# Attention and two gated MLPs in one kernel: streamed sums of squares, normalisations placed earlier in the schedule, and the first loads of v on another queue

## The chip, the cores and the metric

One Trainium2 chip, one core of it. The metric is the time of one execution on the device in microseconds (us). A measurement gives the median of several runs; a profiled execution gives a span, the granted clock of the matrix engine, and a row for every instruction.

## The reference

Causal attention with a decay bias for 4 batches x 8 heads, 576 positions, head size 64, then a gated MLP behind an RMS normalisation, then a second gated MLP without one. Everything is float32; the tokens are 2304, the model width 512, the hidden width 1536.

```python
scores = scale * q @ k.T                      # per batch and head, scale = 1/8
cum = cumsum(maximum(s, 0))
bias = -(cum[:, None] - cum[None, :])
scores = where(causal, -1e9, scores + minimum(bias, 0))
attn = exp(scores - max(scores)); attn /= sum(attn) + 1e-9
x = (attn @ v)                                # then heads side by side: 2304 x 512
xn = x / sqrt(mean(x * x) + 1e-6) * rms_g
h = silu(xn @ w_gate) * (xn @ w_val); x = h @ w_out
h = silu(x @ w2_gate) * (x @ w2_val); out = h @ w2_out
```

## The kernel before

The program writes no fixed order of instructions by hand. Each step is registered with `op(engines, cost in ns, function, what it reads, what it writes, priority)`. `Plan.run` then plays the whole kernel through once with these costs: each engine takes the ready step with the lowest priority value, a step that lists several engines goes to one of them, and the order that comes out is the order in which the instructions of each engine stand in the program. On the chip the engines follow that order; a step that waits holds up what stands behind it on the same engine. A DMA costs SP 450 ns or bytes / 350 per ns, whichever is more, and its data counts as landed 2300 ns plus bytes / 350 after its start; `later` adds to that for those who need it (2500 ns for the weights).

The engines: PE is the matrix engine, ACT the scalar engine, DVE the vector engine, POOL the general engine, SP the engine that issues nearly all DMAs. ACT can issue DMAs too.

Numbers of float32 are split into two float32r parts, high and low (`H` and `L`), and most products are made as three products of parts. The queries of each batch form two groups: A is positions 0 to 255, B is 256 to 575.

The stages that the change touches lie in the first 460 us or so:

- `attend_early`: group A of batches 0 and 1, 16 heads (`EarlyUnit`). For each head SP loads q and k (`lq`, L858) and v (`vl`, L866), 128 KB and 64 KB. PE makes scores (L874; L880 adds the bias for the first four heads), DVE and ACT make the exponentials (L669, L680), PE transposes them (L890), ACT or DVE evicts the transposes (`pTA`, L895), PE multiplies with v (L900), and ACT or DVE stores the result in `x` (L905).
- Beside it SP loads the weights of the first MLP in pieces of 512 KB (`raw`, L430). They arrive as 8-byte numbers; ACT (L433), DVE (L435), ACT or POOL (L440, L441) and POOL or DVE (L444) make the two parts of them.
- `attend`: group B of batches 0 and 1, then both groups of batches 2 and 3, with masks on POOL (L657, L761), scores L643, minima on DVE (L669), transposes L712, parts on ACT and DVE (L715, L717) and products with v (L724). The splits of q, k and v (L595, L598, L607) go to POOL or DVE.
- `normalise`, once for each group of each batch, eight times. ACT squares `x` in four pieces `k` of 128 rows, two heads each (L926, into `sq`, two buffers). PE sums the squares of each head for each token (L932): the squares are the stationary operand, 128 tokens at a time, and a two-column selector `half` streams, so a piece takes two matmuls for group A and three for B. DVE makes the factor of each token and head from the sums in 20 small steps (L960 to L994), PE transposes the factors (L998), ACT evicts them (L1001), PE spreads each over the 64 rows of its head with the selector `sel` (L1006), and DVE multiplies `x` by it (L1010). ACT and POOL or DVE split the result (L1013, L1015).
- `moe1`: for 12 pieces of the hidden width and each group, 24 matmuls for gate and value (L1026, `gate_value`), with 256 or 320 columns, then L1033, L1035 and L1038, and a store to `h_d` (L1066). These have a high priority value and fill PE wherever the attention leaves it free.
- `sums_of_rows`: from about 315 us on SP loads rows of `h_d` back (`tb`), DVE makes differences of them (L1310) and SP stores these.

Four banks of PSUM (`mo`) are shared by the gate and value matmuls and the normalisations. From about 460 us on come the output product of the first MLP and the second MLP.

The order around the change is set by the priorities:

```python
normalise(x, "A", tot, P_ATT + len(units))           # in attend_early
...
for g, x, tot in zip(gs, xs, tots):                  # in attend
    normalise(x, g, tot, P_ATT + len(units))
...
moe1([(1, "B", 1)], W1, P_ATT + 36, -1.0e4)
```

Of the kernel before, what the change touches and what calls it, by code (L numbers as in the profile page):

```python
# [43 lines left out]
def f32(ap):  # L44
    return ap.bitcast(F32)
# [34 lines left out]
class Plan:  # L80
# [19 lines left out]

    def op(self, eng, ns, fn, r=(), w=(), pri=0.0, later=0, port=False):

# [7 lines left out]
        if eng == SP:  # L110
            took = ns / self.RATE
            ns = max(450.0, took)
            done = 2300.0 + took - ns
        deps, shared = set(), []
# [186 lines left out]
def tile_kernel(  # L301
# [73 lines left out]

    half = buf("m1", "half", [P, 2], F32)
    sel = buf("m1", "sel", [P, 2 * KD, D], F32R)

    totals = [buf("m1", f"tot{i}", [P, 3, NH], F32) for i in range(4)]


    sq = [buf("m1", f"sq{i}", [P, (320, 384)[i]], F32) for i in range(2)]
    tot3 = [buf("m1", f"tt{i}", [P, NH // 2], F32) for i in range(2)]
    xbuf = [buf("m1", f"x{i}", [P, KD, 320], F32) for i in range(2)]
# [17 lines left out]
    def convert(src, dst, c, stage, y, pri, early=None, after=()):  # L402
# [19 lines left out]
        def whole(dtype=F32):  # L422
# [8 lines left out]
            out=stage().bitcast(U16)[:, :4 * n - 1], in_=src.bitcast(U16)[:, 1:]),  # L431
           r=after, w=[stage], pri=pri if early is None else early, later=2500)
        op(ACT, c_act(n) + 165, lambda en: en.activation(  # L433
# [40 lines left out]
    def setup():  # L474
# [34 lines left out]
        def cumulate(out, n, pri, after=()):  # L509
            rows = NB * NH  # L510
            cum2 = buf("at", "cb0" if after else "cvt0", [rows, S], F32, "cum2")

# [12 lines left out]
        def later():  # L525
            def selectors(en):
                for j in range(2):
                    en.memset(half()[64 * j:64 * j + 64, j:j + 1], 1.0)
                    en.memset(half()[64 * j:64 * j + 64, 1 - j:2 - j], 0.0)
                en.tensor_tensor(  # L530
                    out=sel()[:],
                    in0=ident()[:, 0:NH].rearrange("p (h o) -> p h o", o=1).to_broadcast([P, NH, D]),
                    in1=ident()[:, NH:2 * NH].rearrange("p (h o) -> p h o", o=1).to_broadcast([P, NH, D]),
                    op=ALU.add)
            op([(POOL, 1800), (DVE, 1200)], 0, selectors, r=[ident, "early 1"], w=[half, sel], pri=3.5)

# [290 lines left out]
    class EarlyUnit(Unit):  # L827
# [28 lines left out]
        def load(self, pri):  # L856
# [5 lines left out]
            if not self.first:  # L862
                op(SP, 1024, lambda en: en.dma_start(
                    out=ql()[D:D + 1, 1, 288 * i:288 * i + 256], in_=cumA()[n:n + 1]),
                   r=[cumA, self.rows], w=self.parts[2:], pri=pri, later=1000)
            op(SP, 512 * P, lambda en: en.dma_start(out=self.v(), in_=vp[self.b, self.h, :, 0:2]),  # L866
               w=[self.vl], pri=pri)

# [43 lines left out]

    def normalise(i, g, tot, pri):

# [5 lines left out]
        ps = mo_bank()  # L920

        def squares():
            return ps()[:, :nt * NH].rearrange("p (t h) -> p t h", h=NH)
        for k in range(KD):
            q = sq[k % 2]
            op(ACT, c_act(n) + 35, lambda en, q=q, k=k: en.activation(  # L926
                q()[:, :n], x()[:, k, :n], ACTF.Square),
               r=[(x, (k, 0)), (x, (k, 64))], w=[q], pri=pri)

            def sums(en, q=q, k=k):  # L930
                for c in range(nt):
                    en.matmul(squares()[:, c, 2 * k:2 * k + 2], q()[:, at[c]:at[c] + P], half(),  # L932
                              start=True, stop=True)
            op(PE, 206 * nt, sums, r=[q, half], w=[ps], pri=pri)
        col = ring("m1", "rc", 2, [P, 3, 3], F32)
# [152 lines left out]
    def attend_early(b, x, tot):  # L1088
        for h in range(NH):
# [6 lines left out]
            if u.i == 3:  # L1096
                later()
        normalise(x, "A", tot, P_ATT + len(units))

    def attend(b, gs, xs):  # L1100
# [31 lines left out]
        for g, x, tot in zip(gs, xs, tots):  # L1132
            normalise(x, g, tot, P_ATT + len(units))

# [15 lines left out]
    moe1([(0, "B", 0)], W1, P_MOE + 100, -1.0e4)  # L1150
    moe1([(1, "B", 1)], W1, P_ATT + 36, -1.0e4)
    for b in range(2, NB):
# [681 lines left out]
```

## Time and profile before

| | |
|---|---|
| three runs | 1069.13, 1073.40 and 1074.58 us, median 1073.4 |
| the profiled execution | 1078.08 us, span 1076.3 us |
| mean granted clock of PE | 0.994 of full speed |
| busy: PE, DVE, ACT, POOL | 1051.4, 778.9, 634.4, 234.4 us |
| DMA | 211.16 MB, mean 196 GB/s |

Times below are counted from the span's start. Busy time on PE counts pipelined matmuls, so a row's duration is longer than the distance to the next one; prices of matmuls are therefore read from the chain of waits, where the pieces follow each other without overlap. A float32 matmul that is not split stands in the trace as two records.

### The profile page before, as it was taken

Reading aid. Unit: us, or ns where it says so; the run is one execution under the profiler, and the core shown is the slowest. Engines: PE = TensorE matmul, PEld = TensorE weight load, DVE = VectorE, ACT = ScalarE, POOL = GpSimd, SP = SyncE. Lnnn points to the kernel's source line nnn. Section 1 sums busy time; section 2 is a strip of 40 time slices with the busy share of each in tenths; the row PEclk is TensorE's granted clock in tenths of the full one; section 3 lists DMA queues with packets and bytes.
Section 4 is the critical chain, followed back from the end, with each engine's and each line's share of the span. In section 5 each row is a group of like instructions: output and inputs, shape, how many; then the busy total and the mean of one; then the engine's idle time right before and its main releaser. Section 6 shows DMA issues by size and latency. Waiting matters only on the chain.

```text
span 1076.3 us, 19524 instructions
## 1 busy us (share of the span) xinstructions
PE 1051.4 (98%) x6372; PEld 947.4 (88%) x6372; DVE 778.9 (72%) x1882; ACT 634.4 (59%) x1355; POOL 234.4 (22%) x322
## 2 busy tenths in 40 slices
PE   7989999999998999999999999999999999999998
PEld 5689999999998999999987889888888888878888
DVE  6888887866787876666777889566657776876453
ACT  5879767856762675332455766545556544664552
POOL 4158634522331341000000000122112221200000
PEclk9999999999999999999999999999999999999999
DMA  6786645433447751566588673565766658877773
GB/s 175 256 273 183 182 139 151 145 100 100 122 132 238 231 159 37 188 194 210 186 268 270 204 223 98 192 223 197 247 218 238 234 195 282 284 259 244 229 226 118
DMA packets 127382, 211.16 MB, mean 196 GB/s; under 512 B 16112, under 2 KB 55024, under 8 KB 127280
## 3 DMA queue, kind: packets, MB, share of 16 engines
q1 hardware_dynamic: 127232, 209.84, 61.5%
q8 instruction: 50, 0.82, 0.3%
q14 instruction: 52, 0.43, 0.1%
q10 hardware_dynamic: 48, 0.07, 0.0%
HBM read 145.29 MB, written 64.56 MB: 195 GB/s over the span
## 4 chain that ended last, share of the span: by engine, by line
PE 75%; DVE 10%; DMA 6%; ACT 4%; issue 3%; SPq 1%; POOL 0%; DVEq 0%; ACTq 0%; POOLq 0%
PE mo L1026 20%; PE mo L1565 9%; PE mo L1395 8%; PE sps L1565 7%; PE tp L724 4%; PE tp L1395 4%; PE sps L1395 4%; PE mo L1641 2%; PE tp L712 2%; PE sps L643 2%; PE sps L1026 2%; PE tp L1026 2%; PE mo L1450 2%; DMA raw<-in_w_gv 2%; DMA tb<-h_d 1%
## 5 line engine op out<-in xcount | busy, mean ns | idle before, releaser
L1026 PE MATMUL mo<-xL,H 128*128 128x256 f32 (+1 forms) x672 | 203.1, 302 | 1.1 <-DVE xL L1015 0.9
L1026 PE MATMUL mo<-xH,H 128*128 128x256 f32 (+1 forms) x672 | 202.6, 303 | 0.1
L1026 PE MATMUL mo<-xH,L 128*128 128x256 f32 (+1 forms) x672 | 202.2, 301 | 0.0
L1291 DVE TENSOR_TENSOR hL<-hh,hH 128x512 fp32r<-128x512 f32 (+1 forms) x192 | 124.1, 662 | 74.0 <-ACT hH L1288 73.8
L1288 ACT ACTIVATE hH<-hh 128x512 fp32r<-128x512 f32 (+1 forms) x192 | 114.3, 602 | 94.7 <-DVE hL L1291 13.8
L1026 PEld LDWEIGHTS mo<-xL,H 128*128 128x128 f32 x672 | 128.5, 191 | 1.9 <-DVE xL L1015 1.2
L1026 PEld LDWEIGHTS mo<-xH,H 128*128 128x128 f32 x672 | 128.4, 191 | 0.8 <-ACT xH L1013 0.3
L1026 PEld LDWEIGHTS mo<-xH,L 128*128 128x128 f32 x672 | 128.5, 191 | 0.1
L680 ACT ACTIVATE sc<-sc,col 128x128 f32<-128x128 f32 (+3 forms) x128 | 73.1, 572 | 58.3 <-DVE col L669 57.4
L1395 PE MATMUL mo<-hH,wo 128*128 128x512 f32 x312 | 98.1, 390 | 0.4 <-ACT hH L1288 0.4
L1395 PEld LDWEIGHTS mo<-hH,wo 128*128 128x128 f32 x312 | 58.6, 188 | 13.1 <-ACT hH L1288 1.1
L1033 ACT ACTIVATE t<-mo 128x256 f32<-128x256 f32 (+1 forms) x84 | 34.0, 405 | 59.9 <-PE mo L1026 59.6
L1395 PE MATMUL mo<-hL,wo 128*128 128x512 f32 x156 | 61.1, 391 | 0.6 <-DVE hL L1291 0.4
L1395 PE MATMUL tp<-hH,wo 128*128 128x512 f32 x192 | 60.4, 389 | 0.0
L1035 DVE SCALAR_TENSOR_TENSOR t<-t,mo 128x256 f32<-128x256 f32 (+1 forms) x84 | 37.9, 451 | 30.7 <-ACT t L1033 30.1
L1571 ACT ACTIVATE u<-sps 128x512 f32<-128x512 f32 x48 | 28.5, 594 | 51.7 <-PE sps L1565 49.8
L724 PE MATMUL tp<-pTB,vst 128*128 128x320 f32 (+2 forms) x320 | 52.4, 295 | 2.1 <-DVE pTB L717 1.4
L1395 PE MATMUL sps<-hH,wo 128*128 128x512 f32 x168 | 53.2, 390 | 0.5 <-ACT hH L1288 0.5
L724 PEld LDWEIGHTS tp<-pTB,vst 128*128 128x128 f32 x320 | 46.5, 189 | 5.0 <-DVE pTB L717 3.7
L717 DVE TENSOR_TENSOR pTB<-tp,pTB 128x512 fp32r<-128x512 f32 x64 | 44.0, 688 | 8.6 <-ACT pTB L715 7.7
L1038 DVE TENSOR_TENSOR hh<-t,mo 128x256 f32<-128x256 f32 (+1 forms) x84 | 37.8, 450 | 14.7 <-PE mo L1026 13.3
L712 PE MATMUL tp<-ident,sc 128*128 128x128 f32 x304 | 47.1, 274 | 0.2 <-DVE park L798 0.2
(272 smaller groups left out, 2861.8 us busy)
## 6 DMA issues: line engine op xcount, KB each, us to landing
raw<-in_w_gv SPq DMA_DIRECT2D x44, 511.8 KB, 5.3
tb<-h_d SPq DMA_DIRECT2D x48, 256.0 KB, 3.5
t<-tb SPq DMA_DIRECT2D x48, 256.0 KB, 2.2
hh<-t SPq DMA_DIRECT2D x48, 256.0 KB, 3.2
lq<-in_qk SPq DMA_DIRECT2D x32, 288.0 KB, 3.6
cb<-cum_d SPq DMA_DIRECT2D x32, 288.0 KB, 3.6
hh<-h_d SPq DMA_DIRECT2D x36, 256.0 KB, 3.3
h_d<-hh SPq DMA_DIRECT2D x54, 128.0 KB, 2.2
```

Source lines behind the costliest of these rows:

```text
L680: op(ACT, c_act(o + m, 2) + 35, lambda en: en.activation(sc()[:m, :o + m], sc()[:m, :o + m], ACTF.Exp, scale=-1.0, bias=col()[:m, 0, t:t + 1],
L712: op(PE, C_TR, lambda en, pt=pt, a=a, kb=kb, t=t: en.transpose(pt()[:, a * P:a * P + P], self.sc[t]()[:, kb * P:kb * P + P], ident()), r=[ ...
L717: op(DVE, c_tt(n), lambda en, pt=pt, c=c: en.tensor_tensor(out=place(L, c), in0=source(pt, c), in1=f32(place(H, c)), op=ALU.subtract), r=[ ...
L724: op(PE, c_mm(n), lambda en, w=w, z=z, kb=kb, d0=d0, n=n, o=o: en.matmul(po()[:, o:o + n], vst[j]()[:, kb, :], pT[g][z]()[:, d0:d0 + n], s ...
L1026: op(PE, c_mm(n), lambda en, a=a, x=x, c=c, k=k, i=i: en.matmul(ps()[:, :n], a()[:, c], x()[:, k, :n], start=(k == 0 and i == 0), stop=(k ...
L1033: op(ACT, c_act(n), lambda en: en.activation(t()[:, :n], gp()[:, :n], ACTF.Tanh, scale=0.5), r=[gp], w=[t], pri=pri)
L1035: op(DVE, c_tt(n), lambda en: en.scalar_tensor_tensor(out=t()[:, :n], in0=t()[:, :n], scalar=1.0, in1=gp()[:, :n], op0=ALU.add, op1=ALU.mu ...
L1038: op(DVE, c_tt(n), lambda en: en.tensor_tensor(out=hh()[:, :n], in0=t()[:, :n], in1=vp_()[:, :n], op=ALU.mult), r=[vp_, t], w=[hh], pri=pri)
L1288: op(ACT, c_act(n) + 35, lambda en: en.activation(H(), src(), ACTF.Copy), r=[src, *after], w=[H], pri=pri)
L1291: lambda en: en.tensor_tensor(out=L(), in0=src(), in1=f32(H()), op=ALU.subtract),
L1395: op(PE, c_mm(n), lambda en, m=m, w=w, xx=xx, kk=kk, i=i: en.matmul(ps[m]()[:, :n], w(), xx(), start=first and kk == 0 and i == 0, stop=kk ...
L1565: op(PE, c_mm(n), lambda en, w=w, xx=xx, cut=cut, kk=kk, i=i: en.matmul(ps()[:, :n], W[w]()[:, cut], xx(), start=first and kk == 0 and i == 0,
```

## The change

Six of the eight normalisations (all but those of `attend_early`) sum the squares in another way. Each piece of squares is split into a high part (`sqH`, on POOL or ACT) and a low part (`sqL`, on DVE or POOL). The parts stream through PE, with a window of the selector `zsel` as the stationary operand: 72 columns wide, of which only the two columns of this piece's heads hold ones. Eight matmuls of 256 or 320 columns add up in one bank, eight heads by tokens; ACT or DVE evicts the sums, PE transposes them into a second bank, 128 tokens at a time, and the small steps go on from there. `zsel` is made in `selectors`.

Every normalisation's priority value is lowered by 2, that of group A in `attend` by 1 more, and that of the gate and value work of batch 1, group B, is raised from 36 to 40. The loads of v of the first four early heads are issued by ACT's queue, ahead of everything else there but the load of s. The schedule counts the weights of the first five pieces (ten transfers) as landing 1500 ns later.

```diff
-    def op(self, eng, ns, fn, r=(), w=(), pri=0.0, later=0, port=False):
+    def op(self, eng, ns, fn, r=(), w=(), pri=0.0, later=0, port=False, slow=0.0):
...
-            done = 2300.0 + took - ns
+            done = 2300.0 + took - ns + slow
...
+    zsel = buf("m1", "zsel", [P, 72 + 2 * KD - 2], F32R)
+    sqs = buf("ex", "ex2", [P, 1024], F32R, "sqs")
+    sqH = [Part(sqs, i, lambda t, i=i: t[:, 320 * i:320 * i + 320]) for i in range(2)]
+    sqL = Part(sqs, 2, lambda t: t[:, 640:960])
...
-           r=after, w=[stage], pri=pri if early is None else early, later=2500)
+           r=after, w=[stage], pri=pri if early is None else early, later=2500,
+           slow=0.0 if early is None or early > P_ATT - 986 else 1500.0)
...
+                en.memset(f32(zsel()), 0.0)
+                for j in range(2):
+                    en.memset(f32(zsel()[64 * j:64 * j + 64, 2 * KD - 2 + j:2 * KD - 1 + j]), 1.0)
...
-            op(SP, 512 * P, lambda en: en.dma_start(out=self.v(), in_=vp[self.b, self.h, :, 0:2]),
-               w=[self.vl], pri=pri)
+            if self.first:
+                op(ACT, 450, lambda en: en.dma_start(
+                    out=self.v(), in_=vp[self.b, self.h, :, 0:2]), w=[self.vl], pri=pri - 1e6)
+            else:
+                op(SP, 512 * P, lambda en: en.dma_start(
+                    out=self.v(), in_=vp[self.b, self.h, :, 0:2]), w=[self.vl], pri=pri)
...
-    def normalise(i, g, tot, pri):
+    def normalise(i, g, tot, pri, split=True):
+        pri -= 2
...
-            def sums(en, q=q, k=k):
-                for c in range(nt):
-                    en.matmul(squares()[:, c, 2 * k:2 * k + 2], q()[:, at[c]:at[c] + P], half(),
-                              start=True, stop=True)
-            op(PE, 206 * nt, sums, r=[q, half], w=[ps], pri=pri)
+            if not split:
+                def sums(en, q=q, k=k):
+                    for c in range(nt):
+                        en.matmul(squares()[:, c, 2 * k:2 * k + 2], q()[:, at[c]:at[c] + P], half(),
+                                  start=True, stop=True)
+                op(PE, (206 * nt, 2), sums, r=[q, half], w=[ps], pri=pri)
+                continue
+            qh = sqH[k % 2]
+            op([(POOL, c_pts(n)), (ACT, c_act(n) + 35)], 0, {
+                ACT: lambda en, q=q, qh=qh: en.activation(qh()[:, :n], q()[:, :n], ACTF.Copy),
+                POOL: lambda en, q=q, qh=qh: en.tensor_scalar(
+                    out=qh()[:, :n], in0=q()[:, :n], scalar1=1.0, scalar2=1.0, op0=ALU.mult,
+                    op1=ALU.mult)}, r=[q], w=[qh], pri=pri)
+            op([(DVE, c_tt(n)), (POOL, c_ptt(n))], 0, lambda en, q=q, qh=qh: en.tensor_tensor(
+                out=sqL()[:, :n], in0=q()[:, :n], in1=f32(qh()[:, :n]),
+                op=ALU.subtract), r=[q, qh], w=[sqL], pri=pri, port=True)
+
+            def sums(en, qh=qh, k=k):
+                for z, part in enumerate((qh, sqL)):
+                    en.matmul(ps1()[:72, :n], zsel()[:, 2 * (KD - 1 - k):2 * (KD - 1 - k) + 72],
+                              part()[:, :n], start=k + z == 0, stop=k + z == KD)
+            op(PE, 2 * c_mm(n), sums, r=[qh, sqL, zsel], w=[ps], pri=pri)
+        if split:
+            op([(ACT, c_act(n)), (DVE, c_tt(n))], 0, {
...
+               r=[ps], w=[sq[0]], pri=pri)
+            ps2 = mo_bank()
+            for c in range(nt):
+                op(PE, C_TR, lambda en, c=c: en.transpose(
+                    ps2()[:, c * P:c * P + P], sq[0]()[:, at[c]:at[c] + P], ident()),
+                   r=[sq[0], ident], w=[ps2], pri=pri)
+            ps = ps2
...
-        normalise(x, "A", tot, P_ATT + len(units))
+        normalise(x, "A", tot, P_ATT + len(units), False)
...
-            normalise(x, g, tot, P_ATT + len(units))
+            normalise(x, g, tot, P_ATT + len(units) - (1.0 if g == "A" else 0.0))
...
-    moe1([(1, "B", 1)], W1, P_ATT + 36, -1.0e4)
+    moe1([(1, "B", 1)], W1, P_ATT + 40, -1.0e4)
```

How it moves the instructions is shown at three places. The line numbers of the changed kernel are larger: L866 is the load of `lq` there, L875 that of `vl` on ACT, L434 that of the weights, L950 the sums as before, L966 the streamed sums, L1051 the spreading with `sel`, L1071 gate and value.

First the start of SP's queue, before the change from its fifth transfer on (ahead of it stands the same pair of `lq` and `vl` twice):

```order
L858 DMA lq_118<-in_qk 64x2x256
L866 DMA vl_122<-in_vp 128x128
L858 DMA lq_110<-in_qk 64x2x256
L866 DMA vl_146<-in_vp 128x128
L430 DMA raw_168<-in_w_gv 128x2047
L858 DMA lq_118<-in_qk 64x2x256
L430 DMA raw_180<-in_w_gv 128x2047
```

and now from its third on (ahead of it two loads of `lq`):

```order
L866 DMA lq_118<-in_qk 64x2x256
L866 DMA lq_110<-in_qk 64x2x256
L434 DMA raw_152<-in_w_gv 128x2047
L434 DMA raw_168<-in_w_gv 128x2047
L866 DMA lq_118<-in_qk 64x2x256
L434 DMA raw_180<-in_w_gv 128x2047
```

The loads of `vl`, four among the first eight transfers, are gone, and the first load of weights stands fifth instead of ninth.

The same time on ACT, up to the second conversion of weights (`cvy`), before:

```order
L480 DMA cum<-in_s 32x576
L680 ACT_TABLE_LOAD
L680 ACTIVATE sc_172,tot_126<-sc_172,col_173 128x128
L680 ACTIVATE sc_182,tot_126<-sc_182,col_173 128x256
L680 ACTIVATE sc_188,tot_126<-sc_188,col_189 128x128
L433 ACTIVATE cvy<-raw_168 128x512
L895 ACTIVATE pTA_208<-tp_186 128x384
L433 ACTIVATE cvy<-raw_180 128x512
```

and now, from the third of four loads of `vl` on, the load of `cum` ahead of them all:

```order
L875 DMA vl_122<-in_vp 128x128
L875 DMA vl_141<-in_vp 128x128
L688 ACT_TABLE_LOAD
L688 ACTIVATE sc_174,tot_127<-sc_174,col_175 128x128
L688 ACTIVATE sc_184,tot_127<-sc_184,col_175 128x256
L688 ACTIVATE sc_190,tot_127<-sc_190,col_191 128x128
L438 ACTIVATE cvy<-raw_152 128x512
L907 ACTIVATE pTA_209<-tp_188 128x384
L438 ACTIVATE cvy<-raw_168 128x512
```

The four loads of `vl` stand ahead of the table load; the eviction `pTA` of the first head still stands behind the first conversion of weights.

The third place is PE in the normalisations of the last batch, from the spreading of group A on (`sel`), with group B's sums of squares beside it, before:

```order
L1026 MATMUL mo_6300<-xH_1384,L_535 128x320
L1006 MATMUL mo_6324<-xL_638,sel 128x256
L1006 MATMUL mo_6326<-xL_638,sel 128x256
L932 MATMUL mo_5945<-half,sq_124 128x2 x3
L932 MATMUL mo_5945<-half,sq_304 128x2 x3
L1006 MATMUL mo_6348<-xL_638,sel 128x256
L1006 MATMUL mo_6351<-xL_638,sel 128x256
L932 MATMUL mo_5945<-half,sq_124 128x2 x3
L1026 MATMUL mo_6361<-xH_1384,H_612 128x320
L1026 MATMUL mo_6361<-xL_1327,H_612 128x320
```

and now:

```order
L1071 MATMUL mo_6434<-xH_1297,L_733 128x320
L1051 MATMUL mo_6464<-xL_642,sel 128x256
L1051 MATMUL mo_6468<-xL_642,sel 128x256
L966 MATMUL mo_6365<-sqs,zsel 72x320 x2
L1051 MATMUL mo_6477<-xL_642,sel 128x256
L1071 MATMUL mo_6486<-xH_1297,H_808 128x320
L1071 MATMUL mo_6486<-xL_1245,H_808 128x320
L1071 MATMUL mo_6486<-xH_1297,L_879 128x320
```

Before, nine sums with two columns (`half`) stand between and behind the four spreading matmuls; now there are two streamed sums (`zsel`) between them, and the next two pairs follow after 14 and 19 more gate and value matmuls.

## Rows read from the trace of the kernel before

**Rows 1.** Busy us by stretch: PE, PEld, DVE, ACT, POOL; then clock, DMA share, GB/s.

```profile
0.00:60.00 60.00, 50.58 (x271) 38.40 (x272) 46.40 (x162) 45.33 (x127) 18.96 (x33) 0.95 0.75 226
60.00:90.00 30.00, 28.18 (x219) 27.35 (x218) 25.37 (x87) 23.40 (x55) 19.86 (x25) 0.99 0.83 261
60.00:400.00 340.00, 331.00 (x2496) 323.16 (x2495) 268.96 (x898) 230.91 (x577) 144.70 (x229) 0.99 0.55 164
```

**Rows 2.** Who PE waited for, whole span: us in total, times, longest us.

```profile
PE sps L874 <- POOL mask L504: 3.8, 1, 3.8
PE tp L900 <- ACT pTA L895: 3.6, 2, 2.4
PE mo L1006 <- DVE hh L1038: 1.8, 1, 1.8
PE mo L932 <- ACT sq L926: 1.2, 1, 1.2
```

**Rows 3.** Busy us by stretch, three stretches in which the granted clock is low.

```profile
57.00:60.60 3.60, 3.60 (x18) 3.60 (x18) 3.54 (x11) 2.98 (x7) 0.82 (x1) 0.53 0.99 321
343.60:347.20 3.60, 3.53 (x17) 3.53 (x18) 3.06 (x8) 0.89 (x3) 0.00 (x0) 0.54 0.60 224
431.50:435.00 3.50, 3.50 (x19) 3.50 (x19) 2.60 (x13) 1.39 (x5) 0.67 (x1) 0.66 0.84 277
```

**Rows 4.** Line 932, its matmuls: duration ns min/median/max, first and last start.

```profile
L932 PE MATMUL mo<-half,sq x160: 165/251/272, 22.0 to 431.6; 128*128 128x2 f32 x160
```

**Rows 5.** The chain that ended last: start us, us, what, instructions.

```profile
289.42 0.79 PE mo L932 x8
349.14 0.44 PE tp L712 x4
349.58 0.34 PE mo L932 x4
...
479.92 3.52 PE mo L1026 x24
513.83 2.88 PE tp L1026 x24
```

**Rows 6.** Timeline of the start, SP's queue, then ACT: start us, us, instruction.

```profile
0.73 0.68 SPq L858 DMA_DIRECT2D lq<-in_qk  x1
5.75 0.43 SPq L430 DMA_DIRECT2D raw<-in_w_gv  x1
...
1.14 1.28 ACT L680 ACT_TABLE_LOAD   x1 [1.14 <-PEq L1824]
5.93 0.40 ACT L680 ACTIVATE sc<-sc,col 128x128 f32<-128x128 f32 x1 [3.50 <-DVE col L669]
11.60 0.77 ACT L433 ACTIVATE cvy<-raw 128x512 f16<-128x512 bf16 x1 [2.75 <-DMA raw<-in_w_gv]
12.25 0.46 ACT L895 ACTIVATE pTA<-tp 128x384 f32<-128x384 f32 x1
```

**Rows 7.** Busy us by stretch at the start.

```profile
3.00:4.50 1.50, 0.68 (x2) 0.50 (x2) 1.44 (x2) 0.00 (x0) 1.31 (x4) 1.00 0.52 146
10.50:12.70 2.20, 0.00 (x0) 0.00 (x0) 0.95 (x6) 1.10 (x2) 0.00 (x0) 1.00 1.02 321
12.70:16.20 3.50, 3.44 (x9) 2.37 (x10) 1.92 (x2) 2.37 (x8) 1.94 (x2) 0.51 0.30 103
```

**Rows 8.** Tiles `raw` (the weights' transfers) in the first 70 us, issue to landing.

```profile
DMA to landing us min/median/max: 3.9/5.3/7.3
```

**Rows 9.** Timeline of DVE in batch 2's normalisations.

```profile
333.66 1.42 DVE L1310 TENSOR_TENSOR tb<-tb 128x512 f32<-128x512 f32 x2 [2.22 <-DMA tb<-h_d]
```

**Rows 10.** Groups by line and form on POOL: count, busy us, mean ns, idle before.

```profile
L595 POOL TENSOR_TENSOR qst<-lq,qst 64x640 fp32r<-64x640 f32 x5 | 8.1, 1628 | 6.2 <-issue 5.3 <-ACT qst L593 0.6
L1015 POOL TENSOR_TENSOR xL<-x,xH 128x320 fp32r<-128x320 f32 x10 | 9.1, 926 | 51.9 <-ACT xH L1013 51.9
```

More of the change, by code (lines that the diff above doesn't have):

```diff
@@ L510, in cumulate @@
             rows = NB * NH
-            cum2 = buf("at", "cb0" if after else "cvt0", [rows, S], F32, "cum2")
+            cum2 = buf("at", "cb0" if after else "cvt0", [rows, n], F32, "cum2")
             def steps(en):
@@ L534, in selectors @@
                     op=ALU.add)
-            op([(POOL, 1800), (DVE, 1200)], 0, selectors, r=[ident, "early 1"], w=[half, sel], pri=3.5)
+            op([(POOL, 1800), (DVE, 1200)], 0, selectors, r=[ident, "early 1"], w=[half, zsel, sel], pri=3.5)
             def clear_scores(en):
@@ L920, in normalise @@
         ps = mo_bank()
+        ps1, ps2 = ps, None
         def squares():
+            if split:
+                return ps2()[:, :nt * P].rearrange("p (t h) -> p t h", h=P)[:, :, :NH]
             return ps()[:, :nt * NH].rearrange("p (t h) -> p t h", h=NH)
@@ L928, in normalise @@
                r=[(x, (k, 0)), (x, (k, 64))], w=[q], pri=pri)
-            def sums(en, q=q, k=k):
-                for c in range(nt):
-                    en.matmul(squares()[:, c, 2 * k:2 * k + 2], q()[:, at[c]:at[c] + P], half(),
-                              start=True, stop=True)
-            op(PE, 206 * nt, sums, r=[q, half], w=[ps], pri=pri)
+            if not split:
[19 more added lines that the diff above has]
+            op(PE, 2 * c_mm(n), sums, r=[qh, sqL, zsel], w=[ps], pri=pri)
+        if split:
+            op([(ACT, c_act(n)), (DVE, c_tt(n))], 0, {
+                ACT: lambda en: en.activation(sq[0]()[:72, :n], ps1()[:72, :n], ACTF.Copy),
+                DVE: lambda en: en.tensor_copy(sq[0]()[:72, :n], ps1()[:72, :n])},
+               r=[ps], w=[sq[0]], pri=pri)
[5 more added lines that the diff above has]
+            ps = ps2
         col = ring("m1", "rc", 2, [P, 3, 3], F32)
```

## Prediction, made blind

> **What bounds the kernel now.** I read the busy times by stretch first, then who PE waits for, then the start on SP, ACT and the DMA engines, then the chain of waits for what PE's work costs. PE is busy for 331.00 of the 340 us from 60 to 400 us, and for only 50.58 of the first 60 [rows 1]. So the kernel is bound by the amount of work on PE, and idle time is worth looking for at the start: 9.4 us there, 9.0 us in the next 340. PE's instructions stand in a fixed order, so a wait for a late operand is lost for good, whatever other work is ready behind it. The waits of PE [rows 2] name four places: 3.8 us before the first matmul, two waits of L900 for `pTA` (3.6 us, the longer 2.4, so the other 1.2), one of 1.8 us of the spreading matmul L1006 for DVE, and one of 1.2 us of the sums of squares (L932) for ACT. The stretches at half clock [rows 3] are a second loss, which no list of waits shows: a mean of 0.53 over 3.6 us means that 1.7 us of work's time was lost there.
>
> **The change part by part**, against the profiled execution (1078.1 us, span 1076.3); it stands 4.7 us above the median of the three runs, 1073.4, and I carry the difference over to that median.
>
> *Sums of squares.* L932 has 160 records, two for each of 80 instructions [rows 4]. The two early normalisations keep theirs (2 x 4 x 2 = 16 instructions), so 64 instructions, 128 records, go. In the chain of waits four records take 0.34 us and eight take 0.79 [rows 5], 0.085 to 0.099 each; with 0.09 this is 11.5 us of PE. Added are 48 matmuls with a 72-column weight: 32 that stream 320 columns and 16 that stream 256. Streaming them costs, by the gate and value matmuls (L1026) of the same operand types, 3.52 / 24 = 0.147 and 2.88 / 24 = 0.120 us [rows 5], so 4.7 + 1.9 us, and 16 transposes at 0.44 / 4 = 0.11 us [rows 5] make 1.8. Added: 8.4. Net **-3.1 us**, all of it on the path, since PE is the bound; -2.5 and -4.3 by the two prices of a record.
>
> *The first v from ACT's queue.* SP issued its first transfer at 0.73 and its ninth, the first weights, at 5.75 [rows 6]: 0.63 us each. With four transfers of v gone the weights are the fifth, at about 3.25, 2.5 us sooner. They matter at once, because ACT's first conversion of weights (L433, waiting for them until 11.60) stands ahead of the eviction `pTA` (12.25), for which PE waits: PE has no busy time at all from 10.5 to 12.7 [rows 6, 7]. A weight transfer lands 3.9 to 7.3 us after its issue, median 5.3 [rows 8]; from 3.25 that is 8.6, the conversion and the eviction follow in 1.2 us, and the eviction then waits for nothing but its transposes. PE goes on at about 10.5: **-2.2 us**; with 7.3 us of flight it is 11.7, -1.1. The idle time is also followed by half clock (0.51 from 12.7 to 16.2 [rows 7]), 1.7 us lost; without the gap I expect half of that back, **-0.9** (0 to -1.7). On ACT the four issues (some 0.6 us each, as on SP) come between that of `cum` and the load of the activation table. That load takes 1.28 us, and the first exponential starts at 5.93 [rows 6]: 1.14 + 2.4 + 1.28 = 4.8, hidden with 1.1 us to spare. The Trainium skill (ScalarE: Activation LUTs, What ACT_TABLE_LOAD costs) has 2.66 us for a load with its drain, and by that figure the exponential would be late by an estimated 0.3 us. No row here shows the drain, and the row's 1.28 stands in the sum.
>
> *Longer first transfers in the schedule.* This moves nothing in time by itself; it places the conversions of the first ten transfers where their data really is there (counted 1.5 us later, near the median flight above). What it can mend is L900's second wait of 1.2 us, also behind a conversion whose weights were late. I take **-0.8** (0 to -1.2).
>
> *Normalisations ranked ahead.* Before, the second early normalisation's last two sums stand together on PE behind their squares, wait 1.2 us [rows 2], and half clock follows from 57.0 to 60.6 (1.7 us [rows 3]); now they are apart, with gate and value matmuls between. The squares can also be late in the new places: **-1.4** (0 to -2.9). In the last batch nine instructions of the two-column kind and four spreading matmuls stand nearly in a row, and the clock falls behind them without any wait (0.66 from 431.5 to 435.0 [rows 3]); that costs 0.34 x 3.5 = 1.2 us. The order rows show them now spread among gate and value matmuls that stream 320 columns: **-1.2** (0 to -1.2).
>
> *Batch 2.* There the eight spreading matmuls of both groups still stand in a run, with all gate and value work before them used up, and DVE, in order, still has differences of rows ahead of them that wait for a transfer (2.22 us before 333.66 [rows 9]). What was lost (1.8 us of waiting, 1.7 at half clock [rows 2, 3]) may come again, go, or double: **0** (-3.5 to +3.5).
>
> *The longer chain.* A square is now copied on POOL or ACT and subtracted on DVE or POOL before PE may use it, and the sums are evicted and transposed. All of that lies beside gate and value matmuls unless PE reaches it too early; then what is queued behind on PE waits too. The trace has no such operation. The nearest row is L932's wait of 1.2 us [rows 2]: one for each of the six streamed normalisations would be 7.2, none is the other end, and I take **+2**, since the order leaves such matmuls between a square and its sums.
>
> Sum: -3.1 - 2.2 - 0.9 - 0.8 - 1.4 - 1.2 + 0 + 2 = -7.6. From 1073.4 this is 1065.8, so **1066 us**. All best ends give 1056, all worst 1081. From the last normalisation on the order is unchanged on every engine, so I expect that part only to start earlier.
>
> **The rivals.**
> *The DMA engines, not the queue, set when the weights land.* Then three terms (-2.2, -0.9, -0.8) vanish and -3.7 is left: 1069.7. For it: the DMA engines are full just before PE goes on (321 GB/s, share 1.02 [rows 7]). Against it: while SP was issuing the small transfers they moved only 146 GB/s at half their share [rows 7]. The Trainium skill speaks for this rival (DMA: Bandwidth & Descriptors, Issuing engines are not separate DMA queues): a second issuing engine saves only the sequencer's time of issue, which it calls usually small beside the transfer. At 0.63 us for 64 to 128 KB this trace does not agree with "small".
> *The chain of the streamed sums is late each time.* With the 7.2 us above in place of 2 the sum is -2.4: 1071. For it: DVE does 20 small steps in each normalisation and is busy for 25.37 of 30 us from 60 to 90 [rows 1]. Against it: PE's list shows a single wait for squares now.
> *POOL's new work slows DVE: slower.* By the order POOL has 8 more differences of q, 4 of v, 13 of squares and 12 copies, while DVE gives up the first twelve. At 1.63 and 0.93 us [rows 10] they are at most 8 x 1.63 + 29 x 0.93 = 40 us. If DVE were held up for as long, it would go from 269 to 309 busy us of the 340 [rows 1], 91%. From 60 to 90 us it stands at 85%, and PE is idle for 6% (1.8 of 30 [rows 1]); 6% of 340 is 20.6 us instead of 9.0. That is +11.6 in place of my +2: net +2.0, and with three more falls of the clock at 1.7 us, +7: 1081. It decides once DVE's share passes some 85%. Against it: DVE is at 79% over the long stretch, and what went to POOL was taken from it.
>
> **How the numbers follow.** About 0.5% (5.4 us) is what a measurement of this kernel can tell from no change: 1068.0 and 1078.8 are the bounds. My forecast gets 0.60; it lies 2 us beyond the lower bound, and its terms are mostly bounded at zero. The transfers' rival gets 0.17, the late chain 0.15, both within the bounds. POOL gets 0.08. So faster 0.60, same 0.32, slower 0.08. The range from 1058 to 1075 takes in both rivals in the middle and most of the better ends; it leaves out the worst ends with POOL's case, and the case that every gain is had in full.
>
> **What would show it.** Right: PE starts L900 near 10.5 us and no half clock follows; the first weights land before 9.5; the streamed sums take 0.15 us each and PE's busy time falls by 3 us or more; PE's idle time in the first 60 us falls from 9.4 to about 5; the clock stays full in the last batch. Wrong: the first weights still land near 11.6; PE waits for `sqs` or for the transposes of the sums, 1 us at a time; DVE's share rises over 85% beside POOL; or the sums with the 72-column weight take more than 0.15 us each.

## The result, and the profile after

The changed kernel takes 1061.72 us (median of six runs, 1057.80 to 1065.54) against 1073.28 for the kernel before (six runs, 1069.13 to 1079.21): ratio 0.989, 95% interval 0.9864 to 0.9917, so 11.6 us less. The forecast was 7.3 less, with a range that holds the result. The profiled execution after took 1061.81 us, span 1060.0, right at its median; that of before stands 4.8 above its own, so the two traces differ by 16.3.

The windows of the kernel after, with the columns of [rows 1]:

```profile
0.00:60.00 60.00, 52.84 (x321) 41.86 (x321) 49.93 (x163) 46.22 (x129) 24.05 (x46) 1.00 0.84 248
60.00:400.00 340.00, 332.14 (x2478) 323.30 (x2479) 270.85 (x919) 241.55 (x609) 168.12 (x254) 0.99 0.54 161
300.00:380.00 80.00, 75.82 (x555) 72.26 (x553) 63.43 (x201) 44.97 (x116) 34.85 (x51) 0.98 0.70 210
327.50:333.50 6.00, 5.77 (x25) 4.59 (x25) 6.00 (x15) 3.37 (x8) 2.94 (x4) 0.72 0.51 167
425.00:440.00 15.00, 14.94 (x101) 14.61 (x101) 11.77 (x37) 7.13 (x14) 2.35 (x3) 1.00 0.75 233
```

In the first 60 us PE is idle for 7.2 us instead of 9.4, and the clock is full there (0.95 before [rows 1]). From 60 to 400 it is idle for 7.9 instead of 9.0. The last batch's spreading (425 to 440) runs at full clock; a fall is left in batch 2. DVE's share from 60 to 400 is 79.7% (79.1% before), POOL has 23 us more.

Who PE waited for, after (columns of [rows 2]):

```profile
PE sps L886 <- DMA lq<-in_qk: 4.0, 1, 4.0
PE tp L732 <- DVE pTB L725: 1.4, 3, 0.9
PE tp L912 <- ACT pTA L907: 1.3, 2, 1.0
PE mo L966 <- DVE sqs L960: 0.5, 1, 0.5
```

The waits for `pTA` (L912, formerly L900) are down from 3.6 to 1.3 [rows 2]; the wait for the squares (1.2 [rows 2]) has become one of 0.5 for a part of them (`sqs`). The start, on SP's queue, on ACT and on PE (columns of [rows 6]):

```profile
0.73 2.60 SPq L866 DMA_DIRECT2D lq<-in_qk  x4
3.86 1.26 SPq L434 DMA_DIRECT2D raw<-in_w_gv  x2
...
1.14 2.29 ACTq L875 DMA_DIRECT2D vl<-in_vp  x4
3.47 1.28 ACT L688 ACT_TABLE_LOAD   x1 [3.47 <-DMA cum<-in_s]
6.42 0.40 ACT L688 ACTIVATE sc<-sc,col 128x128 f32<-128x128 f32 x1 [1.67 <-DVE col L677]
10.17 0.78 ACT L438 ACTIVATE cvy<-raw 128x512 f16<-128x512 bf16 x1 [0.82 <-DMA raw<-in_w_gv]
10.81 0.46 ACT L907 ACTIVATE pTA<-tp 128x384 f32<-128x384 f32 x1
...
11.33 0.86 PE L912 MATMUL tp<-pTA,vl 128*64 128x256 f32 x4 [1.05 <-ACT pTA L907]
```

SP issues the first weights at 3.86 instead of 5.75, ACT converts them at 10.17 instead of 11.60, and PE goes on at 11.33 instead of 12.7 [rows 6, 7]. Of 1.9 us gained at the issue 1.4 arrive. Three signs of the prediction were thus missed: PE going on near 10.5, weights landed before 9.5 and some 5 us of idle time in the first 60; the clock in the last batch came as said.

**An account of PE's time.** Waits and clock falls are mixed in these views, so I also took the distance from each matmul's start to the next one's, for all 14 kernels of this study, one trace each. The usual distance of a form (its tiles and its shape; the median over all kernels) counts as work, what is over it as loss: waiting, half clock and gaps. Work is 1031.8 us with the two-column sums everywhere, 1025.8 with the streamed ones. What lies outside the matmuls is 7.3 to 8.3 us in each. The ratio goes by the means of runs made beside the kernel before, so it can differ a little from that of the medians. S, V, C, R are the parts in a kernel: streamed sums, v from ACT's queue, counted transfers, ranks.

| kernel | parts | median us | ratio (95%) | span | loss 0–60 | 60–300 | 300–380 | 380–end |
|---|---|---|---|---|---|---|---|---|
| before | none | 1073.28 | 1 | 1076.3 | 10.7 | 7.9 | 10.2 | 8.3 |
| c1 | none, reordered | 1068.91 | 0.9975 (0.9955–0.9996) | 1068.7 | 8.8 | 8.6 | 2.9 | 9.0 |
| d1 | none, reordered | 1075.21 | 1.0010 (0.9991–1.0028) | 1070.4 | 9.5 | 10.9 | 5.1 | 5.7 |
| c2 | R | 1067.07 | 0.9955 (0.9935–0.9976) | 1062.9 | 7.7 | 7.7 | 2.0 | 6.3 |
| c3 | VC | 1066.56 | 0.9947 (0.9925–0.9969) | 1064.3 | 4.6 | 4.4 | 8.9 | 6.8 |
| c4 | S | 1068.98 | 0.9968 (0.9951–0.9986) | 1066.0 | 9.3 | 9.9 | 5.5 | 8.0 |
| d4 | CR | 1063.70 | 0.9908 (0.9889–0.9927) | 1061.9 | 7.7 | 6.0 | 2.0 | 7.0 |
| e1 | VCR | 1060.35 | 0.9882 (0.9858–0.9905) | 1057.6 | 4.6 | 7.0 | 2.3 | 4.1 |
| e2 | SCR | 1058.69 | 0.9867 (0.9843–0.9891) | 1057.0 | 7.8 | 6.6 | 6.7 | 2.8 |
| e3 | SVR | 1060.54 | 0.9885 (0.9862–0.9908) | 1060.4 | 13.8 | 4.9 | 5.8 | 2.6 |
| e4 | SVC | 1060.19 | 0.9880 (0.9858–0.9903) | 1057.1 | 4.5 | 7.7 | 5.9 | 4.9 |
| after | SVCR | 1061.72 | 0.9890 (0.9864–0.9917) | 1060.0 | 4.7 | 7.6 | 9.6 | 4.7 |
| d2 | SVCR, reordered | 1070.75 | 0.9980 (0.9964–0.9996) | 1065.9 | 4.6 | 11.9 | 9.7 | 6.2 |
| d3 | SVCR, reordered | 1064.64 | 0.9920 (0.9904–0.9937) | 1064.9 | 5.6 | 8.7 | 9.8 | 6.9 |

### The profile page after: what moved, and what is told of

It reads as the page before. It is cut to its first block, busy times and chain, and to the rows that moved or that the text cites. A ratio compares the mean times of both kernels' runs of the same rounds, so it can differ in the third digit from the quotient of the medians.

```text
span 1060.0 us, 19434 instructions
## 1 busy us (share of the span) xinstructions
PE 1039.3 (98%) x6308; PEld 937.0 (88%) x6308; DVE 782.2 (74%) x1881; ACT 642.8 (61%) x1375; POOL 262.4 (25%) x360
## 4 chain that ended last, share of the span: by engine, by line
PE 58%; DVE 3%; DMA 3%; ACT 1%; issue 1%; SPq 0%; ACTq 0%; DVEq 0%
PE mo L1610 10%; PE mo L1071 9%; PE sps L1610 9%; PE mo L1440 8%; PE tp L1440 5%; PE sps L1440 5%; PE mo L1686 3%; PE sps L1071 2%; PE tp L1071 2%; PE mo L1495 2%; PE tp L1610 1%; PE sps L1495 1%; PE tp L1495 1%; DVE hL L1336 1%; DMA hh<-h_d 1%; PE tp L732 1%
## 5 line engine op out<-in xcount | busy, mean ns | idle before, releaser
L1071 PE MATMUL mo<-xL,H 128*128 128x256 f32 (+1 forms) x672 | 201.5, 300 | 0.9 <-DVE xL L1060 0.9
L1071 PE MATMUL mo<-xH,H 128*128 128x256 f32 (+1 forms) x672 | 201.2, 301 | 0.3 <-DVE hh L1083 0.2
L1071 PE MATMUL mo<-xH,L 128*128 128x256 f32 (+1 forms) x672 | 200.7, 300 | 0.0
L1336 DVE TENSOR_TENSOR hL<-hh,hH 128x512 fp32r<-128x512 f32 (+1 forms) x192 | 126.3, 669 | 69.8 <-ACT hH L1333 69.0
L1071 PEld LDWEIGHTS mo<-xL,H 128*128 128x128 f32 x672 | 127.5, 190 | 1.9 <-DVE xL L1060 1.1
L1071 PEld LDWEIGHTS mo<-xH,H 128*128 128x128 f32 x672 | 127.3, 190 | 1.2 <-ACT xH L1058 0.7
L1071 PEld LDWEIGHTS mo<-xH,L 128*128 128x128 f32 x672 | 127.3, 190 | 0.1
L1625 ACT ACTIVATE u<-u 128x512 f32<-128x512 f32 x48 | 29.6, 631 | 29.6 <-DVE u L1620 29.5
```

Source lines behind the costliest of these rows:

```text
L1071: op(PE, c_mm(n), lambda en, a=a, x=x, c=c, k=k, i=i: en.matmul(ps()[:, :n], a()[:, c], x()[:, k, :n], start=(k == 0 and i == 0), stop=(k ...
L1336: lambda en: en.tensor_tensor(out=L(), in0=src(), in1=f32(H()), op=ALU.subtract),
```

## The experiments

### One part undone

Four kernels take one part out of the kernel after.

**e1: two-column sums again.** Their cost in the schedule stays `(206 * nt, 2)`; that form alone moves no instruction of the kernel before.

```diff
-    def normalise(i, g, tot, pri, split=True):
+    def normalise(i, g, tot, pri, split=False):
```

> The changed kernel with the two-column sums in all eight normalisations; v on ACT's queue, the longer first transfers and the ranking stay. Theory (the gain is a sum of parts): 64 two-column sums come back at 0.18 us and 8.4 us of streamed work go, +3.1 us, and a fall of the clock comes back behind the last batch's sums, +1.2 to 1.7: about 1066 us against 1061.7 of the whole change, and a stretch near 425 to 440 us with a granted clock under 0.9. Rival (the ranking, not the new sums, is what helps in the last batch): +3.1 alone or less, clock full there, 1062 to 1065. Rival (the order that the schedule happens to find decides): any time from 1058 to 1073, and waits of PE in places that have nothing to do with the sums.

**e2: v of the first four heads from SP again.**

```diff
-            if self.first:
-                op(ACT, 450, lambda en: en.dma_start(
...
+            op(SP, 512 * P, lambda en: en.dma_start(out=self.v(), in_=vp[self.b, self.h, :, 0:2]),
+               w=[self.vl], pri=pri)
```

> The changed kernel with the first four loads of v back on SP's queue, all else as changed. Theory: the first weights are issued near 5.8 us instead of 3.9 and land near 11.6 instead of 10.2, the first product with v starts at 12.8 instead of 11.3, and half clock comes back behind it (mean about 0.5 from 12.7 to 16.2): +1.4 + 1.7 = +3.1 us, about 1064.8. Rival (the DMA engines set the landing): the weights land as in the changed kernel, no change of time, 1061.7. Rival (chance order): first 20 us as the theory says, the end anywhere from 1058 to 1070.

**e3: the first transfers counted as before.**

```diff
-           slow=0.0 if early is None or early > P_ATT - 986 else 1500.0)
+           slow=0.0 if early is None or early > P_ATT - 986 else 0.0)
```

> The changed kernel without the 1500 ns for the first ten weight transfers in the schedule. Theory: a conversion of weights stands again before its data is there on ACT, one wait of PE for pTA of about 1.2 us near 35 to 45 us comes back: +0.8 to +1.2 us, about 1062.7. Rival: the flight time was not what placed the waits, no change within 0.2%. Rival (chance order): off by more than 3 us either way with the same first 20 us.

**e4: the old ranks.**

```diff
-        pri -= 2
...
-            normalise(x, g, tot, P_ATT + len(units) - (1.0 if g == "A" else 0.0))
+            normalise(x, g, tot, P_ATT + len(units))
...
-    moe1([(1, "B", 1)], W1, P_ATT + 40, -1.0e4)
+    moe1([(1, "B", 1)], W1, P_ATT + 36, -1.0e4)
```

> The changed kernel with the old priorities (no 2 less for normalisations, no 1 less for group A, 36 in place of 40). Theory: the last two sums of the second early normalisation stand together again behind late squares, 1.2 us of wait and 1.7 us at half clock near 55 to 60 us; the last batch keeps its full clock thanks to the streamed sums: +2.9, about 1064.6. Rival (the ranking mends the last batch too): another fall of the clock near 430 us, +4.5, 1066. Rival (chance order): any time from 1058 to 1070.

All four lie at 1058.7 to 1060.5 with overlapping intervals, none above the kernel after. None of the four theories' times (1066, 1064.8, 1062.7, 1064.6) came, and by the median no part carries the gain. The stretches tell more.

In e2 the first weights are issued at 5.72 as expected, but the first product with v starts at 11.38 and not at 12.8, and no half clock follows: with the longer counts the schedule has put the eviction `pTA` ahead of the first conversion of weights. ACT and PE of e2:

```profile
10.84 0.49 ACT L903 ACTIVATE pTA<-tp 128x384 f32<-128x384 f32 x1 [1.49 <-PE tp L898]
11.22 0.77 ACT L438 ACTIVATE cvy<-raw 128x512 f16<-128x512 bf16 x1
11.38 0.86 PE L908 MATMUL tp<-pTA,vl 128*64 128x256 f32 x4
```

In e4 neither the wait nor the half clock expected near 55 to 60 us came, and in the last batch both e4 (streamed sums, old ranks) and e1 (ranks, two-column sums) keep the full clock. Two windows of e4, then one of e1:

```profile
55.00:60.00 5.00, 5.00 (x41) 4.89 (x41) 4.76 (x21) 4.65 (x11) 4.83 (x8) 1.00 0.99 328
425.00:440.00 15.00, 14.99 (x103) 14.47 (x102) 12.46 (x36) 7.65 (x16) 2.81 (x4) 1.00 0.75 240
425.00:440.00 15.00, 15.00 (x105) 15.00 (x104) 10.63 (x35) 5.41 (x11) 0.69 (x1) 1.00 0.64 193
```

Without the streamed sums (e1) PE has 6.0 us more work and the same time, because less is lost from 300 to 380 us, the stretch with batch 2's normalisations and the first half of the last batch's attention (called batch 2 below). The window from 300 to 380 of e1, against 75.82 busy us and clock 0.98 after:

```profile
300.00:380.00 80.00, 79.22 (x600) 77.88 (x599) 62.90 (x186) 41.32 (x106) 22.45 (x37) 1.00 0.71 223
```

In e3 v comes from ACT's queue but the schedule believes the weights to be there sooner. The timeline of e3 near 51 us, on ACT and PE, and then the window behind it:

```profile
50.52 0.77 ACT L438 ACTIVATE cvy<-raw 128x512 f16<-128x512 bf16 x1 [2.51 <-DMA raw<-in_w_gv]
51.16 0.46 ACT L907 ACTIVATE pTA<-tp 128x384 f32<-128x384 f32 x1
...
51.68 1.54 PE L912 MATMUL tp<-pTA,vl 128*64 128x256 f32 x4 [2.14 <-ACT pTA L907]
```

```profile
51.60:61.00 9.40, 9.32 (x40) 8.59 (x41) 7.67 (x20) 7.55 (x18) 4.83 (x5) 0.50 0.82 257
```

ACT waits 2.51 us for weights with the eviction `pTA` behind that conversion, PE waits 2.14, and 9.4 us at 0.50 follow, the lower of the clock's two levels (1.2 and 2.4 GHz). The first 60 us lose 13.8, more than in any other kernel, though the median (1060.54) is not worse.

### One part alone, and a new order of the kernel before

**c1** changes no part: one number in the schedule, the cost of a transpose, which puts the instructions in another order.

```diff
-C_TR = 110
+C_TR = 112
```

> The kernel before with none of the parts of the change: only the number by which the schedule counts one transpose is 112 instead of 110, which computes the same and puts the instructions in another order from early in the program on. Theory A (the parts of the change each take away a loss of their own or share one, and the order as such is worth nothing): 1071 to 1075 us, ratio to the kernel before 0.999 to 1.002. Theory B (the order of the kernel before is an unlucky one, and any new order loses less): 1059 to 1066 us, ratio below 0.994.

**c2** has the ranks alone, **c3** the two parts at the start, **c4** the streamed sums (their diffs are the lines shown above, put into the kernel before).

> The kernel before with the new ranks alone (normalisations 2 ahead, group A's 1 more, and 40 for 36). Theory A (parts share a loss and add up in part): by the prediction's terms 2.6 us are its own, so 1069 to 1071 us, with the half-clock window of the last batch's spreading (431 to 435 us) gone and that of 57 to 61 us still there. Theory B (any new order): 1059 to 1066 us like the reordered kernel. Theory C (each part alone takes away the same whole loss): 1060 to 1063 us while the reordered kernel stays at 1072.

> The kernel before with the two parts at the start alone: the first four heads' v issued from ScalarE's queue, and the first weights' transfers counted as 1500 ns longer. By the terms of the prediction 3.9 us are its own. Theory A: 1066 to 1070 us, first product of the first batch's v some 1.4 us earlier and no half clock at 57 to 61 us, the fall of the clock at 431 to 435 us still there. Theory B: 1059 to 1066 us like the reordered kernel. Theory C: 1060 to 1063 us with the reordered kernel at 1072.

> The kernel before with the streamed sums of squares alone (for the same groups as in the change); v, the counts of the transfers and the ranks as before. By the terms of the prediction 3.1 us less work on TensorE. Theory A: 1068 to 1071 us, TensorE busy 3 us less or more, start as before (first product of v at 12.8 us). Theory B: 1059 to 1066 us like the reordered kernel. Theory C: 1060 to 1063 us with the reordered kernel at 1072.

The reordering gained 0.25%, 2.7 us, by itself: theory B is wrong as put (not below 0.994), but theory A's "worth nothing" as well. The sums alone (0.9968) can't be told from it; ranks and start give 0.45 and 0.53%, and their intervals overlap that of c1 as well. By time c3 and c4 are in theory A's ranges and c2, whose trace has no fall of the clock, is 2 us below its own. Each single part stays well above the four kernels with three parts, so C falls. PE's timeline at the start of c1, then windows of c1:

```profile
11.91 0.86 PE L900 MATMUL tp<-pTA,vl 128*64 128x256 f32 x4 [2.46 <-ACT pTA L895]
```

```profile
12.00:16.00 4.00, 3.38 (x18) 2.46 (x19) 2.11 (x11) 2.75 (x9) 2.17 (x3) 1.00 0.67 192
56.00:61.00 5.00, 5.00 (x42) 5.00 (x42) 4.65 (x16) 3.82 (x9) 1.61 (x3) 1.00 0.90 270
340.00:350.00 10.00, 9.37 (x77) 9.17 (x78) 7.58 (x20) 3.87 (x10) 2.85 (x3) 1.00 0.68 230
424.00:431.00 7.00, 7.00 (x44) 6.89 (x43) 4.64 (x17) 2.90 (x8) 0.73 (x1) 0.76 0.77 227
568.00:576.00 8.00, 6.77 (x21) 5.20 (x22) 6.96 (x12) 4.50 (x8) 0.00 (x0) 0.79 0.83 246
```

The wait is as long as before (2.46 against 2.4 [rows 2]), but no half clock follows here, where 0.51 did before [rows 7]; the falls at 57 and 344 us [rows 3] are gone, that of the last batch is still there (0.76), and one at 568 us is new.

### How much of it is the order

**d1** is the kernel before with `C_TR = 108`, **d2** and **d3** are the kernel after with 112 and 108. **d4** has ranks and counts, without streamed sums and with v on SP: the two undoings that lay lowest, in one kernel.

> The kernel before with nothing of the change, reordered in a second way: one transpose is counted as 108 instead of 110. The first reordering gave 1068.9 against 1072.5. Theory D (what a new order is worth is chance, of some 4 us to either side of a mean near 1069, through the falls of the clock and waits that it happens to have): 1066 to 1073 us, with another set of half-clock stretches than the kernel before and the first reordering have. Theory E (the order of the kernel before is the only bad one, and every other has 1069): 1068 to 1070 us.

> The kernel after, reordered in the same way as the first time: one transpose counted as 112, the whole change kept. Theory D (the change is worth some 8 us and chance orders lie about that): 1058 to 1065 us, mean of both reorderings near 1061. Theory F (the order of the kernel after is a lucky one, and the change itself is worth only the 3 to 5 us that its parts show alone): 1064 to 1068 us.

> The kernel after, reordered in the second way: one transpose counted as 108, the whole change kept. Theory D: 1058 to 1065 us. Theory F: 1064 to 1068 us. By both, the time over that of the undisturbed order goes with the sum of PE's idle time and of the time lost at half clock in its profile, not with PE's work, which stays at some 1036 us at full clock.

> The kernel before with the ranks and the longer counts of the first transfers, without the streamed sums and with v on SP: the two undoings that lay lowest (1058.7 and 1060.4), together. If any two parts are enough to take the whole gain: 1059 to 1062 us. If the parts add up: the ranks alone gave -5.5 and the start's two parts together -6.0, of which the counts alone can have anything from 0 to all, so 1061 to 1067 us. If v's queue and the streamed sums both matter: 1066 to 1068 us, like the ranks alone.

The same change in three orders is at 0.989, 0.998 and 0.992 of the kernel before; that kernel in three orders at 1, 0.9975 and 1.001. One order is thus worth up to 9 us (1061.72 to 1070.75) with nothing else changed. Theory E falls with d1. Of theory D the spread holds, but not the values: d1 (1075.2) and d2 (1070.8) are above its bounds, and the two reorderings of the kernel after lie at 1067.7 in the mean, not near 1061. That mean is in F's band (1064 to 1068), though d2 by itself is above it too: the order of the kernel after is a lucky one among these three. The last sentence expected of d3 (time goes with the losses, work stays) holds for the spans: 1060.0, 1065.9, 1064.9 with losses of 26.6, 32.4, 31.0; the account has the work fixed, so this says only that what lies outside the matmuls hardly moved. The mean of the three ratios is 0.9930 with the change and 0.9995 without: 0.65%, 7 us; by the two reorderings with the change alone (0.9950) it is 4.8. With so few orders that is a coarse number: some 5 to 7 us. d4 is at 1063.7, above the 1059 to 1062 of "any two parts are enough" and inside the 1061 to 1067 of "the parts add up"; its interval, from 1060.7 on, doesn't tell the two apart. e1, which has v from ACT's queue besides, is 3.3 lower, with intervals that overlap.

Some losses don't hang on the order. In the first 60 us the kernels with V and C lose 4.5 to 5.6 us (six kernels), those with C alone of the two 7.7 and 7.8, the one with V alone 13.8, those with neither 7.7 to 10.7. In batch 2 (300 to 380) the kernels with ranks and two-column sums lose 2.0 to 2.3 (c2, d4, e1), the whole change 9.6 to 9.8 in all three orders; e2 and e3, which have ranks and streamed sums too, lose 6.7 and 5.8. The windows of c2 and of d2 there:

```profile
300.00:380.00 80.00, 79.53 (x601) 78.30 (x601) 62.78 (x183) 39.50 (x100) 20.51 (x33) 1.00 0.69 220
```

```profile
300.00:380.00 80.00, 74.81 (x546) 70.74 (x545) 62.88 (x193) 43.36 (x109) 28.27 (x42) 1.00 0.71 216
```

PE does 4.7 us less in the same 80, at full clock in both; POOL has 7.8 us more to do and ACT 3.9, DVE the same.

## Why the prediction came out, point by point

**The sum** (-7.6) is nearer to the mean over orders (5 to 7 us less) than to the pair it was made for (11.6 less). The rest of the pair's difference goes to the order, for which the prediction had no term; that the pair came out inside the range owes something to luck. Between the means of three profiles each (1071.8 and 1063.6, -8.2) the account has: work -6.0, first 60 us -4.7, 60 to 380 +3.9, behind 380 -1.7, together -8.5; the other 0.3 lies outside the matmuls. The forecast's terms for the same places were -3.1, -5.3, +2 and -1.2: the sum is near because 2.9 us more work saved and 1.9 us more lost nearly cancel.

**Sums of squares, -3.1: mis-sized, -6.0.** The added matmuls cost what was taken. The step that failed is the price of a two-column record, "with 0.09". The timeline of PE, before, around the eight records whose chain row [rows 5] gave 0.79:

```profile
289.26 0.95 PE L932 MATMUL mo<-half,sq 128*128 128x2 f32 x8
290.07 0.39 PE L1026 MATMUL mo<-xH,H 128*128 128x320 f32 x1
290.30 0.31 PE L1026 MATMUL mo<-xL,H 128*128 128x320 f32 x1
```

The matmul behind them takes 0.23 us to the next start instead of 0.147, and the chain books that on L1026. From 289.26 to 290.30, less 0.147, is 0.89 for eight: 0.112 each, 14.3 us for 128. The streamed sums and their transposes, timeline of PE after:

```profile
430.79 0.45 PE L966 MATMUL mo<-sqs,zsel 128*72 128x320 f32 x2
431.08 0.32 PE L1071 MATMUL mo<-xH,H 128*128 128x320 f32 x1
...
433.44 0.49 PE L976 MATMUL mo<-ident,sq 128*128 128x128 f32 x3
433.68 0.39 PE L1071 MATMUL mo<-xL,H 128*128 128x320 f32 x1
433.91 0.31 PE L1071 MATMUL mo<-xH,L 128*128 128x320 f32 x1
```

Two streamed matmuls take 0.29 us, three transposes 0.47 - 0.147 = 0.32. By the median distances (0.147, 0.117, 0.108) the additions are 4.7 + 1.9 + 1.7 = 8.3, and 8.3 - 14.3 is -6.0.

**The first v and the longer counts, -2.2, -0.9, -0.8: the sum about right, the split wrong.** Added to the ranks both take 3.1 us off the first 60 us (7.7 to 4.6, c2 and e1), added to nothing 5.1 (9.7, the mean of the three orders, to 4.6 in c3). But "-0.8" for the counts and -3.1 for v as terms of their own are not there: counts without v give nothing in the sum (7.7 in d4 as in c2), v without counts costs 6 (13.8 in e3; one kernel, so its half clock may be chance). Nor is v's queue needed to take away the first wait: with the counts alone of the two, e2 (rows above) and d4 (10.65) start the first product without it, and lose as much later. Sooner weights move the schedule's early steps; where it still counts on data that is not there, PE meets later conversions instead of the first. PE went on at 11.33, not 10.5: the weights were issued at 3.86 (3.25 forecast) and ACT had them 6.3 us after the issue, against 5.3 taken. No half clock followed, 1.7 us less than in the trace before. But c1, d1, c2 and c4, all with v on SP and with PE waiting at this place, have a clock of 1.00 from 12.7 to 16.2 as well, so the clock's term isn't shown to be the change's.

The rival of the DMA engines fell: an earlier issue did bring the weights sooner, though 0.5 us of 1.9 was lost on the way. The Trainium skill's rule (DMA: Bandwidth & Descriptors, Issuing engines are not separate DMA queues) that such a step saves only the time of issue agrees with this trace; that this time is small does not, with four issues at 0.65 us each. On ACT the four issues took 2.29 us and the table load 1.28 again; the first exponential waited for DVE, not for the table. A second table load, later in the kernel after, shows the price without such a wait:

```profile
666.30 1.28 ACT L1625 ACT_TABLE_LOAD   x1
667.65 1.23 ACT L1625 ACTIVATE u<-u 128x512 f32<-128x512 f32 x2
```

The next instruction starts 0.07 us behind it. The Trainium skill's 2.66 us for a load with its drain (ScalarE: Activation LUTs, What ACT_TABLE_LOAD costs) does not agree with these rows, and the measured 1.28 decides.

**Normalisations ranked ahead, -1.4 and -1.2.** At the start the ranks alone give -2.0 (9.7 to 7.7), but taken out of the whole they cost nothing there (4.5 in e4, 4.7 after), so -1.4 is no term of its own. In the last batch three of the four kernels with neither ranks nor streamed sums have the fall (before, c1, c3; d1 has not), and none of the ten with either: each of the two parts goes with its absence. What it costs was read from a window that ends before the fall does; at 0.50 from 432.6 to 436.0 it is 1.7 us, not 1.2. What the prediction lacked: with two-column sums the ranks save some 4 us in batch 2 (2.0 to 2.3 against 2.9, 5.1 and 10.2).

**Batch 2, 0, and the longer chain, +2.** Against the one trace before, 0 was right (10.2 lost there, 9.6 after), and for the reason given: the eight spreading matmuls stand in a run behind DVE's differences of rows again. DVE and PE after, then PE of e1, where they stand in two groups of four 17 us apart:

```profile
327.14 3.02 DVE L1055 SCALAR_TENSOR_TENSOR x<-x,gcol,mo 128x320 f32<-128x320 f32 x7
327.28 2.12 PE L1051 MATMUL mo<-xL,sel 128*128 128x256 f32 x5 [0.61 <-DVE hh L1083]
...
331.46 0.40 PE L1051 MATMUL mo<-xL,sel 128*128 128x256 f32 x2
```

In a run each spreading matmul starts only some 0.4 us behind the other, as fast as DVE multiplies (3.02 / 7 = 0.43). From 325 to 335 us the kernel after loses 4.4; e1 loses 0.8 and 0.6 at its two groups.

Against the other kernels this is where the work saved goes. In batch 2 the whole change loses 9.7 us against 2.3 in e1, 7.4 more for 6.0 saved. Only part of the rest is named: of the list's waits of 0.5 us and more in this stretch, which add up to 3.4, the spreading has one, the attention the others. The added POOL and ACT work (rows of c2 and d2 above) makes a longer chain the likely cause. For it: with the eight parted, the kernels with streamed sums still lose 5.5 to 9.8 here (c4, d3, e2, e4), those without 2.0 to 5.1 (c1, c2, d1, d4, e1). It was not isolated, nor told apart from the second of the four `mo` banks that each streamed sum takes. The late-chain rival ("1 us at a time") comes near in size by luck only: in the trace after, PE waited for the squares once, for 0.5 us.

**POOL slows DVE: fell.** POOL got 23 us more from 60 to 400, DVE's share moved from 79.1 to 79.7%.

**Open.** Whether the change without streamed sums is better than the whole: e1 and after are equal within their intervals, and none of the kernels with a part undone was reordered. No kernel was shown to beat the one after; e2's interval (0.9843 to 0.9891) overlaps its own.

## What to carry to other kernels

Where a planner sets the order, one neutral change of a cost is a control that belongs in every comparison: here it moved the time by up to 9 us, more than any single part did, and a part undone in one order proves little by the median; the losses of a stretch, over several kernels, do. Price a short matmul to the second start behind it, since what it delays is booked on its neighbour. An edit that makes data come sooner belongs together with the schedule's own estimate of that transfer: the one trace that had v sooner without the estimate (e3) lost 13.8 us in the first 60, the kernel after 4.7.

## What the runs showed that was not expected

Half clock is not a fixed consequence of a wait: waits of 2.39 and 2.46 us at the same place were followed by 0.51 in the kernel before [rows 7] and by 1.00 in c1. It also differs between executions of one kernel: of d1's twelve one of 1068.83 us had a mean clock of 1.000 and one of 1078.84 had 0.990. 1% of 1070 us is 10.7, about the difference; but a third, of 1076.86, had 0.997, so the clock is not all of it.

The first matmuls are slow though the clock's column says 1.00 there (its record begins 8.7 us into the span). The same two matmuls on PE after, early and later:

```profile
5.71 1.06 PE L886 MATMUL sps<-lq 128*128 128x256 f32 x2
12.29 0.60 PE L886 MATMUL sps<-lq 128*128 128x256 f32 x2
```
